# Block transposes on VectorE and moves by DMA in place of TensorE transposes, in the second layer of an attention and two-layer expert kernel

## The chip, the cores and the metric

The kernel runs on one core of a Trainium2 chip. Its time is the device time of one execution in microseconds; the median of three runs is the number that is compared. The engines of the core are called TensorE (PE in the profile; PEld is its loading of stationary operands), VectorE (DVE), ScalarE (ACT), GpSimd (POOL) and SyncE (SP, which here only issues DMAs).

## The reference

A chunked attention (4608 tokens, 8 heads of 64) gives x of 4608 x 512. A first layer with a cosine gate follows, and then the second layer, the one that is changed. All values are float32.

```python
def _moe_ref(x, w_in, w_out):            # 512 -> 2048 -> 512
    h = x @ w_in
    g = h * np.cos(h)
    return (g @ w_out).astype(np.float32)

def _moe2_ref(x, w_in, w_out, g_ln):     # 512 -> 1024 -> 512
    h = x @ w_in
    h_max = np.max(h, axis=-1, keepdims=True)
    e = np.exp(h - h_max)
    sm = e / (np.sum(e, axis=-1, keepdims=True) + 1e-09)
    solu = h * sm
    mu = np.mean(solu, axis=-1, keepdims=True)
    var = np.mean((solu - mu) ** 2, axis=-1, keepdims=True)
    ln = (solu - mu) / np.sqrt(var + 1e-06) * g_ln
    return (ln @ w_out).astype(np.float32)
```

## The kernel before

Products are made of float32 numbers split into a high part `hi` (type float32r) and a low part `lo`; a product is three matmuls, hi by hi, hi by lo, lo by hi. `split` (L115 to L124) makes the high part with a copy on ScalarE and the low part with a subtraction on VectorE.

The attention and the first layer run together in nine blocks of 512 tokens (`NJ` = 9, `T` = 512). The first layer's result y leaves the chip for DRAM (`yd`, L595) and comes back for the second layer (`yr`, L608), with units on partitions and tokens along the row. The second layer's weights are loaded by `load_w2` (L217) and split by `prep_w2` (L228) in the last sixteen steps of the first layer; the gain `gcol`, loaded at L657 among the first loads, is multiplied into the second output weights there (L121, L122).

The second layer goes by tiles of 128 tokens, `NI` = 36 of them, four (`SUB`) to a block. For a tile t:

- `mm_h2(t)` (L812): 24 matmuls make the scores h, 128 tokens on partitions by 1024 units, into one of two two-bank PSUM buffers of `ps_y` (tag y).
- `stats(t)` (L825): on VectorE the maximum `nm` (L829), on ScalarE the exponentials `e` with their sum (L831), on VectorE the units `so` (L836), on ScalarE the sum of squares (L841), on GpSimd the power -1/2 (L846). The last reader of the PSUM buffer is the operation that writes `so`; then `mm_h2(t + 2)` can write it.
- `norm(t)` (L849): one VectorE operation on `so` (L851).
- `mm_t(t)` (L855): eight 128 x 128 transposes of `so` on TensorE into PSUM, `lt` (L861), because the next product needs units on partitions.
- `split_ln(t)` (L864): `lh` and `ll` from `lt`, on ScalarE and VectorE, into tiles of the pool `wp` (32 buffers of 4 KB a partition; the second layer's split weights hold 16 of them).
- `mm_o(t)` (L870): 24 matmuls make 128 tokens by 512 outputs in `ps_h`.
- `store(t)` (L880): a copy on ScalarE, one DMA of 256 KB.

The loop (L887 to L904) writes these in the order `mm_h2(t)`, `norm(t-1)`, `split_ln(t-2)`, `store(t-3)`, `load_y`, `stats(t)`, `mm_o(t-2)`, `mm_t(t-1)`: a tile's output product comes two tiles after its first product. `load_y` (L600) fetches the y of the block after the next one; its destination has two buffers, so it can be split only when the block before the last is through. In this part no order is prescribed for an engine: a planner walks through a simulation of the program and gives each engine the first written operation whose operands and buffers it believes to be ready, and on the chip each engine, SyncE's DMA queue too, keeps the order so found and waits where something is not ready.

Of the kernel before, what the change touches and what calls it, by code (L numbers as in the profile page):

```python
# [11 lines left out]
F32 = mybir.dt.float32  # L12
# [4 lines left out]
AF = mybir.ActivationFunctionType  # L17
# [12 lines left out]
def kernel(  # L30
# [12 lines left out]
    nc = tc.nc  # L43
# [4 lines left out]
    P = 128  # L48
    CH = 64
    T = 512  # L50
    NJ = NT // T
    SUB = T // P
    NI = NT // P
    KD = DM // P
    NF = F1 // P
    NF2 = F2 // P
    NH2 = F2 // 512
# [8 lines left out]
    ps_a = ctx.enter_context(tc.tile_pool(name="ps_a", bufs=1, space=PSUM))  # L66

    ident = const.tile([P, P], F32, name="ident")
    gcol = const.tile([P, NF2], F32, name="gcol")
# [43 lines left out]
    sync = InOrder(nc.sync, in_order_loads)  # L113

    def split(src, hi, lo, mul=None):  # L115

        if mul is None:
            act.activation(out=hi, in_=src, func=AF.Copy)
            dve.tensor_tensor(out=lo, in0=src, in1=hi.bitcast(F32), op=ALU.subtract)
        else:  # L120
            nc.scalar.activation(out=hi, in_=src, func=AF.Copy, scale=mul)  # L121
            nc.vector.scalar_tensor_tensor(  # L122
                out=lo, in0=src, scalar=mul, in1=hi.bitcast(F32), op0=ALU.mult, op1=ALU.subtract
            )  # L124
# [32 lines left out]
    def wtile(dt, name, n=1024):  # L157
        return wp.tile([P, n], dt, tag="w", name=name)
# [13 lines left out]
    def load_one(name, f):  # L172
        t = wtile(U64, "raw", 512)
        load_w(name, f, t)
        raw.setdefault((name, f // 2), []).append(t)

    def load_pair(name, g):
        t = sp_.tile([P, 1024], U64, tag="st", name="st")
        for e in range(2):
            load_w(name, 2 * g + e, t[:, HALVES[e]])  # L180
        raw[name, g] = [t]
# [15 lines left out]
    def prep_split(name, g, e=None):  # L197
        sl = slice(0, 1024) if e is None else HALVES[e]
        if (name, g) not in his:
            his[name, g], los[name, g] = wtile(F32R, "whi"), wtile(F32R, "wlo")  # L200
        split(zs[name, g][:, sl].bitcast(F32), his[name, g][:, sl], los[name, g][:, sl])
        dst = win if name == "in" else wout
        for e in range(2):
            dst[2 * g + e] = tuple(x[name, g][:, HALVES[e]] for x in (his, los))
# [3 lines left out]
    def prep(name, g):  # L208
# [3 lines left out]
        if name == "in" or 2 * g >= N32:  # L212
            prep_split(name, g)

    w2in, w2out = {}, {}

    def load_w2(name, g):  # L217
        t = sp_.tile([P, 1024], U64, tag="st", name="st")
        if name == "in":
            nc.sync.dma_start(out=t, in_=w_in2[g * P:(g + 1) * P, :])  # L220
        else:
            nc.sync.dma_start(
                out=t.rearrange("p (e c) -> p e c", e=2),
                in_=w_out2[2 * g * P:2 * (g + 1) * P, :].rearrange("(e p) c -> p e c", p=P),
            )
        raw[name, g] = t

    def prep_w2(name, g):  # L228
# [371 lines left out]
    def load_y(j, half):  # L600
        if half == 0:
            yh[j] = xp.tile([P, KD, T], F32R, tag="xh", name="yh")
            yl[j] = xp.tile([P, KD, T], F32R, tag="xl", name="yl")
        sl = slice(2 * half, 2 * half + 2)
        ts = []
        for src in y_dram[j]:
            t = sp_.tile([P, 2, T], F32, tag="st", name="yr")
            nc.sync.dma_start(out=t, in_=src[sl].rearrange("m p t -> p m t"))  # L608
            ts.append(t)
        t = ts[0]  # L610
        if len(ts) == 2:
            nc.vector.tensor_tensor(out=t, in0=t, in1=ts[1], op=ALU.add)
        split(t, yh[j][:, sl], yl[j][:, sl])


    def second(r):
        if r < 2:
            load_y(0, r)
        if r == 1:
            load_w2("in", 0)  # L620
        if r < 2 or r % 2:
            return
        g = r // 2 - 1
        order = [("in", x) for x in range(KD)] + [("out", x) for x in range(NF2 // 2)]
        if g < len(order):
            prep_w2(*order[g])
        if g + 1 < len(order):
            load_w2(*order[g + 1])
# [4 lines left out]
    if True:  # L633
# [20 lines left out]
        load_v(SUB)  # L654
        for f in (4, 5):
            load_one("out", f)
        sync.dma_start(out=gcol, in_=g_ln.rearrange("(f p) -> p f", p=P))  # L657
        load_pair("in", 3)

        def tok(i):  # L660
# [98 lines left out]
        for i in range(SUB, NU):  # L759
            j, o = divmod(UNITS[i][0] * CH, T)  # L760
# [48 lines left out]
        sp = ctx.enter_context(tc.tile_pool(name="sp", bufs=2, reuse_waits="tile"))  # L809
        h2ps, solu, nmu, rstd, lnp, lnh, lnl, ops = {}, {}, {}, {}, {}, {}, {}, {}  # L810

        def mm_h2(t):  # L812
            ps = ps_y.tile([P, NH2, 512], F32, tag="y", name="h2")
            j, o = divmod(t, SUB)
            ts = slice(o * P, (o + 1) * P)
            a, b = yh[j][:, :, ts], yl[j][:, :, ts]
            for hh in range(NH2):
                for kk in range(KD):
                    whi, wlo = w2in[kk * NH2 + hh]
                    nc.tensor.matmul(out=ps[:, hh], lhsT=a[:, kk], rhs=whi, start=(kk == 0), stop=False)  # L820
                    nc.tensor.matmul(out=ps[:, hh], lhsT=a[:, kk], rhs=wlo, start=False, stop=False)  # L821
                    nc.tensor.matmul(out=ps[:, hh], lhsT=b[:, kk], rhs=whi, start=False, stop=(kk == KD - 1))  # L822
            h2ps[t] = ps
# [25 lines left out]
        def norm(t):  # L849
            so = solu[t]  # L850
            nc.vector.tensor_scalar(  # L851
                out=so, in0=so, scalar1=nmu.pop(t), scalar2=rstd.pop(t), op0=ALU.add, op1=ALU.mult
            )

        def mm_t(t):  # L855
            so = solu.pop(t).rearrange("p a b -> p (a b)")
            o = ps_a.tile([P, NH2, 4, P], F32, tag="a", name="lt")
            for hh in range(NH2):
                for g in range(4):
                    f = 4 * hh + g  # L860
                    nc.tensor.transpose(out=o[:, hh, g], in_=so[:, f * P:(f + 1) * P], identity=ident)  # L861
            lnp[t] = o

        def split_ln(t):  # L864
            hi, lo = wtile(F32R, "lh"), wtile(F32R, "ll")
            o = lnp.pop(t).rearrange("p a b c -> p (a b c)")
            split(o, hi[:], lo[:])
            lnh[t], lnl[t] = (x.rearrange("p (f c) -> p f c", c=P) for x in (hi, lo))

        def mm_o(t):  # L870
            o = ps_h.tile([P, DM], F32, tag="h", name="o")
            for f in range(NF2):
                a, b = lnh[t][:, f], lnl[t][:, f]
                whi, wlo = w2out[f]
                nc.tensor.matmul(out=o, lhsT=a, rhs=whi, start=(f == 0), stop=False)  # L875
                nc.tensor.matmul(out=o, lhsT=a, rhs=wlo, start=False, stop=False)  # L876
                nc.tensor.matmul(out=o, lhsT=b, rhs=whi, start=False, stop=(f == NF2 - 1))  # L877
            ops[t] = o

        def store(t):  # L880
            s = sp.tile([P, DM], F32, tag="os", name="os")
            nc.scalar.activation(out=s, in_=ops.pop(t), func=AF.Copy)
            nc.sync.dma_start(out=out[t * P:(t + 1) * P, :], in_=s)

        load_y(1, 0)
        load_y(1, 1)
        for t in range(NI + 3):  # L887
            if t < NI:
                mm_h2(t)
            if 0 <= t - 1 < NI:  # L890
                norm(t - 1)
            if 0 <= t - 2 < NI:
                split_ln(t - 2)
            if 0 <= t - 3 < NI:
                store(t - 3)
            if t < NI:
                jn = t // SUB + 2
                if t % SUB >= 2 and jn < NJ:
                    load_y(jn, t % SUB - 2)
                stats(t)  # L900
            if 0 <= t - 2 < NI:
                mm_o(t - 2)
            if 0 <= t - 1 < NI:
                mm_t(t - 1)  # L904


_INS = ["q", "k", "v", "moe_w_in", "moe_w_out", "moe2_w_in", "moe2_w_out", "moe2_g_ln"]
# [24 lines left out]
```

## Time and profile before

| | us |
|---|---|
| median of 3 runs | 1363.74 (1361.95 to 1364.02) |
| profiled execution | 1363.55 |
| its span in the trace | 1361.8 |
| TensorE busy in the span | 1318.3 (97%) |
| VectorE busy | 893.3 (66%) |
| ScalarE busy | 722.2 (53%) |

The table is read from the profiled execution except for its first line. Matmuls are pipelined: one of 512 columns is shown as 390 ns, while at full clock they follow each other every 0.23 us. The second layer begins on TensorE at 928 us. In the trace a name after the line number is the tile that is written, and the names behind the arrow are those that are read; some matmuls carry a wrong tile name among their operands (`whi` for a tile of activations), so the line says which it is.

### The profile page before, as it was taken

How to read it: one execution, taken by the hardware profiler on the slowest of the kernel's cores; microseconds unless marked ns; L12 is line 12 of the kernel's file. 1: busy time of each engine (PE TensorE's matmuls, PEld its weight loads, DVE VectorE, ACT ScalarE, POOL GpSimd, SP SyncE). 2: the span in 40 equal slices, each digit the busy share in tenths (PEclk: the TensorE clock that was granted, in tenths of full speed). 3: DMA queues.
4: the chain of work that ended last, by engine and by line, in shares of the span. 5: the costliest groups of instructions: out<-in, count | busy, mean ns of one | idle time of the engine just before them, and what ended most of it. 6: DMA issues, size and time to landing. Idle time of an engine off the chain costs nothing.

```text
span 1361.8 us, 19898 instructions
## 1 busy us (share of the span) xinstructions
PE 1318.3 (97%) x8048; PEld 1069.0 (78%) x8048; DVE 893.3 (66%) x1326; ACT 722.2 (53%) x1061; POOL 20.5 (2%) x43
## 2 busy tenths in 40 slices
PE   5899999999999999999999999999999999999997
PEld 4566877888888888888888888777888888888886
DVE  4887987666766776677777776997544445444442
ACT  3777886666645554555555455674433344343332
POOL 0000000000000000000000000000000000000000
PEclk9899999999999999999999999999999999999999
DMA  9941343221321221222214003223110111010000
GB/s 239 201 102 62 124 105 66 50 55 22 79 40 23 63 47 31 53 42 46 55 26 105 20 1 115 102 93 124 55 55 24 55 54 55 24 54 18 24 24 31
DMA packets 200172, 87.30 MB, mean 64 GB/s; under 512 B 171408, under 2 KB 179600, under 8 KB 199568
## 3 DMA queue, kind: packets, MB, share of 16 engines
q1 hardware_dynamic: 200080, 86.03, 24.2%
q8 instruction: 63, 1.03, 0.3%
q14 instruction: 29, 0.24, 0.1%
HBM read 65.02 MB, written 20.97 MB: 63 GB/s over the span
## 4 chain that ended last, share of the span: by engine, by line
PE 80%; DVE 9%; ACT 5%; DMA 2%; issue 2%; SPq 1%; POOLq 0%; POOL 0%; ACTq 0%; DVEq 0%
PE h L515 8%; PE y L583 8%; PE y L584 8%; PE h L516 7%; PE y L582 7%; PE h L517 7%; PE o L877 5%; PE o L875 5%; PE o L876 5%; PE h L821 4%; PE h L822 4%; PE h L820 4%; DVE z L105 3%; PE lt L861 2%; PE x L105 2%
## 5 line engine op out<-in xcount | busy, mean ns | idle before, releaser
L515 PE MATMUL h<-xh,whi 128*128 128x512 f32 x576 | 232.6, 404 | 1.0 <-ACT xh L105 1.0
L516 PE MATMUL h<-xl,whi 128*128 128x512 f32 x576 | 226.0, 392 | 1.9 <-DVE xl L105 1.9
L517 PE MATMUL h<-xh,wlo 128*128 128x512 f32 x576 | 226.4, 393 | 0.0
L582 PE MATMUL y<-gh,whi 128*128 128x512 f32 x544 | 211.1, 394 | 10.6 <-ACT gh L105 6.3
L583 PE MATMUL y<-gl,whi 128*128 128x512 f32 x544 | 214.7, 395 | 1.4 <-DVE gl L105 1.3
L584 PE MATMUL y<-gh,wlo 128*128 128x512 f32 x544 | 214.0, 394 | 0.0
L544 ACT ACTIVATE r<-r 128x512 f32<-128x512 f32 x144 | 90.8, 631 | 177.5 <-DVE r L538 177.3
L552 DVE SCALAR_TENSOR_TENSOR hs<-r,hs 128x512 f32<-128x512 f32 x136 | 93.9, 691 | 100.4 <-ACT r L545 100.0
L105 DVE TENSOR_TENSOR gl<-hs,gh 128x512 fp32r<-128x512 f32 x136 | 93.7, 689 | 61.0 <-ACT gh L105 60.7
L582 PEld LDWEIGHTS y<-gh,whi 128*128 128x128 f32 x544 | 102.1, 189 | 35.9 <-ACT gh L105 8.9
L515 PEld LDWEIGHTS h<-xh,whi 128*128 128x128 f32 x576 | 108.9, 189 | 26.2 <-issue 2.2
L516 PEld LDWEIGHTS h<-xl,whi 128*128 128x128 f32 x576 | 108.9, 189 | 25.1 <-DVE xl L105 2.4
L105 ACT ACTIVATE gh<-hs 128x512 fp32r<-128x512 f32 x136 | 85.6, 630 | 80.5 <-DVE hs L552 69.3
L517 PEld LDWEIGHTS h<-xh,wlo 128*128 128x128 f32 x576 | 108.8, 189 | 23.5 <-issue 0.6
L583 PEld LDWEIGHTS y<-gl,whi 128*128 128x128 f32 x544 | 103.1, 189 | 26.1 <-DVE gl L105 4.5
L584 PEld LDWEIGHTS y<-gh,wlo 128*128 128x128 f32 x544 | 103.4, 190 | 21.7 <-DVE wlo L105 0.5
L831 ACT ACTIVATE e<-h,nm 128x1024 f32<-128x1024 f32 x36 | 40.0, 1112 | 144.5 <-DVE nm L829 144.5
L535 DVE SCALAR_TENSOR_TENSOR r<-kt,hs 128x512 f32<-128x512 int32 x144 | 99.4, 690 | 25.2 <-ACT kt L530 21.8
L820 PE MATMUL h<-whi,yh 128*128 128x512 f32 x288 | 114.9, 399 | 0.5 <-DVE so L836 0.5
L875 PE MATMUL o<-whi,lh 128*128 128x512 f32 x288 | 112.3, 390 | 2.2 <-ACT lh L105 2.2
L877 PE MATMUL o<-whi,ll 128*128 128x512 f32 x288 | 112.4, 390 | 1.1 <-DVE ll L105 1.1
L522 ACT ACTIVATE hs<-h 128x512 f32<-128x512 f32 x144 | 85.1, 591 | 53.1 <-PE h L517 44.9
(92 smaller groups left out, 2061.8 us busy)
## 6 DMA issues: line engine op xcount, KB each, us to landing
yd<-ye SPq DMA_DIRECT2D x22, 512.0 KB
yr<-yd SPq DMA_DIRECT2D x22, 512.0 KB
out<-os SPq DMA_DIRECT2D x36, 256.0 KB
vi<-in_v SPq DMA_DIRECT2D x64, 128.0 KB
qi<-in_q SPq DMA_DIRECT2D x224, 32.0 KB
ki<-in_k SPq DMA_DIRECT2D x224, 32.0 KB
st<-in_moe_w_in SPq DMA_DIRECT2D x10, 512.0 KB
st<-in_moe_w_out SPq DMA_DIRECT2D x10, 512.0 KB
```

Of the source, the lines that this page charges most:

```text
L105: ins = getattr(self.engine, name)(*args, **kwargs)
L515: nc.tensor.matmul(out=t, lhsT=wa, rhs=xh[j][:, kk, :], start=(kk == 0), stop=False)
L516: nc.tensor.matmul(out=t, lhsT=wa, rhs=xl[j][:, kk, :], start=False, stop=False)
L517: nc.tensor.matmul(out=t, lhsT=wb, rhs=xh[j][:, kk, :], start=False, stop=(kk == KD - 1))
L535: nc.vector.scalar_tensor_tensor(out=r, in0=kt, scalar=-TWO_PI_HI, in1=h, op0=ALU.mult, op1=ALU.add)
L552: nc.vector.scalar_tensor_tensor(out=gf.get(n, h), in0=rr.pop(n), scalar=-0.5, in1=h, op0=ALU.add, op1=ALU.mult)
L582: nc.tensor.matmul(out=o, lhsT=wa, rhs=a, start=head, stop=False)
L583: nc.tensor.matmul(out=o, lhsT=wa, rhs=b, start=False, stop=False)
L584: nc.tensor.matmul(out=o, lhsT=wb, rhs=a, start=False, stop=last)
L820: nc.tensor.matmul(out=ps[:, hh], lhsT=a[:, kk], rhs=whi, start=(kk == 0), stop=False)
L875: nc.tensor.matmul(out=o, lhsT=a, rhs=whi, start=(f == 0), stop=False)
L877: nc.tensor.matmul(out=o, lhsT=b, rhs=whi, start=False, stop=(f == NF2 - 1))
```

## The change

The eight TensorE transposes of a tile are gone. After `norm(t)`, `blocks32(t)` transposes `so` on VectorE in blocks of 32 x 32: partition 32a + f of the result holds unit f of each of the 32 unit blocks for the 32 tokens of token block a. Four tiles are collected in one tile `bt` (16 KB a partition, one buffer). When the four are complete, `shuffle(j)` moves them with 16 DMAs from SyncE, each from 32 partitions to 32 partitions, 4 KB a row and 128 KB in all: four tiles `lt` arise, each with units on 128 partitions and 128 tokens along the row, taken 32 from each of the four token tiles. `split_ln`, `mm_o` and `store` then work on such a mixed tile (j, a); the split reads SBUF, the output leaves in four DMAs of 32 rows. The units come to lie in another order on the partitions, so the second output weights and the gain are loaded in that order, by four DMAs each in place of one. The output product of a tile comes six tiles after the first product (`LAG2` = 6).

```diff
@@ load_w2 @@
-            nc.sync.dma_start(
-                out=t.rearrange("p (e c) -> p e c", e=2),
-                in_=w_out2[2 * g * P:2 * (g + 1) * P, :].rearrange("(e p) c -> p e c", p=P),
-            )
+            for c in range(4):
+                nc.sync.dma_start(
+                    out=t[32 * c:32 * (c + 1)].rearrange("p (e m) -> p e m", e=2),
+                    in_=w_out2.rearrange("(c q p) m -> c p q m", c=4, p=32)[c, :, 2 * g:2 * g + 2],
+                )
@@ first loads @@
-        sync.dma_start(out=gcol, in_=g_ln.rearrange("(f p) -> p f", p=P))
+        for c in range(4):
+            sync.dma_start(
+                out=gcol[32 * c:32 * (c + 1)],
+                in_=g_ln.rearrange("(c q p) -> c p q", c=4, p=32)[c],
+            )
@@ second layer @@
-        def mm_t(t):
-            so = solu.pop(t).rearrange("p a b -> p (a b)")
-            o = ps_a.tile([P, NH2, 4, P], F32, tag="a", name="lt")
-            for hh in range(NH2):
-                for g in range(4):
-                    f = 4 * hh + g
-                    nc.tensor.transpose(out=o[:, hh, g], in_=so[:, f * P:(f + 1) * P], identity=ident)
-            lnp[t] = o
+        def blocks32(t):
+            j, n = divmod(t, SUB)
+            if n == 0:
+                blks[j] = sp.tile([P, 32, SUB, 32], F32, tag="bt", name="bt", bufs=1)
+            nc.vector.transpose(
+                out=blks[j][:, :, n], in_=solu.pop(t).rearrange("p a (b f) -> p (a b) f", f=32)
+            )
+
+        def shuffle(j):
+            b = blks.pop(j)
+            for a in range(4):
+                l = wtile(F32, "lt")
+                for c in range(4):
+                    nc.sync.dma_start(
+                        out=l[32 * c:32 * (c + 1)],
+                        in_=b[32 * a:32 * (a + 1), 8 * c:8 * (c + 1)].rearrange("p q n t -> p (q n t)"),
+                    )
+                lnp[j, a] = l
...
+        def split_ln(j, a):
             hi, lo = wtile(F32R, "lh"), wtile(F32R, "ll")
+            split(lnp.pop((j, a)), hi[:], lo[:])
...
-        def store(t):
+        def store(j, a):
             s = sp.tile([P, DM], F32, tag="os", name="os")
+            nc.scalar.activation(out=s, in_=ops.pop((j, a)), func=AF.Copy)
+            for n in range(SUB):
+                t0 = j * T + n * P + 32 * a
+                nc.sync.dma_start(out=out[t0:t0 + 32, :], in_=s[32 * n:32 * (n + 1)])
...
-        for t in range(NI + 3):
+        LAG2 = 6
+        for t in range(NI + LAG2 + 1):
             if t < NI:
                 mm_h2(t)
             if 0 <= t - 1 < NI:
                 norm(t - 1)
-            if 0 <= t - 2 < NI:
-                split_ln(t - 2)
-            if 0 <= t - 3 < NI:
-                store(t - 3)
+                blocks32(t - 1)
+                if t % SUB == 0:
+                    shuffle(t // SUB - 1)
+            if 0 <= t - LAG2 + 1 < NI:
+                split_ln(*divmod(t - LAG2 + 1, SUB))
+            if 0 <= t - LAG2 - 1 < NI:
+                store(*divmod(t - LAG2 - 1, SUB))
             if t < NI:
                 jn = t // SUB + 2
                 if t % SUB >= 2 and jn < NJ:
                     load_y(jn, t % SUB - 2)
                 stats(t)
-            if 0 <= t - 2 < NI:
-                mm_o(t - 2)
-            if 0 <= t - 1 < NI:
-                mm_t(t - 1)
+            if 0 <= t - LAG2 < NI:
+                mm_o(*divmod(t - LAG2, SUB))
```

## Rows read from the trace of the kernel before

**Rows 1.** The page's first part: busy time of each engine, share, instructions.
```profile
PE 1318.3 (97%) x8048; PEld 1069.0 (78%) x8048; DVE 893.3 (66%) x1326; ACT 722.2 (53%) x1061; POOL 20.5 (2%) x43
```

**Rows 2.** Stages: length, busy time per engine, granted clock, DMA share, GB/s.
```profile
core 0: us, PE busy (x) PEld busy (x) DVE busy (x) ACT busy (x) POOL busy (x), PEclk, DMA share, GB/s
928.00:1330.00 402.00, 401.18 (x1908) 334.68 (x1907) 197.21 (x333) 152.24 (x226) 18.71 (x35) 1.00 0.13 48
```

**Rows 3.** Chain of waits in the second layer: start, length, what.
```profile
1011.40 0.88 PE lt L861 x8
...
1329.28 0.87 PE lt L861 x8
```

**Rows 4.** Groups by line, 1060 to 1340: busy us, mean ns | idle before.
```profile
L861 PE MATMUL lt<-ident,so 128*128 128x128 f32 x184 | 23.8, 273 | 0.0
```

**Rows 5.** Timeline of VectorE, one tile: start, length, operation, [idle before, releaser].
```profile
1029.54 1.23 DVE L829 TENSOR_REDUCE nm<-h 128x1 f32<-128x1024 f32 x1 [3.17 <-PE h L822]
...
1033.63 0.08 DVE L836 DVE_READ_ACCUMULATOR so<-h,ss,e 128x1 f32 x1
...
1036.17 0.81 DVE L851 TENSOR_SCALAR so<-so,mu,rs 128x1024 f32<-128x1024 f32 x1 [0.73 <-POOL rs L846]
```

**Rows 6.** Line 372, attention: count, shortest/median/longest ns, first and last start.
```profile
L372 DVE STREAM_TRANSPOSE qt<-qi x14: 1235/1236/1240, 162.6 to 769.8; 128x1024 f32<-128x1024 f32 x14
```

**Rows 7.** Groups on VectorE, 1060 to 1340.
```profile
L105 DVE TENSOR_TENSOR ll<-lt,lh 128x1024 fp32r<-128x1024 f32 x24 | 29.3, 1223 | 0.0
L851 DVE TENSOR_SCALAR so<-so,mu,rs 128x1024 f32<-128x1024 f32 x24 | 19.5, 814 | 17.8 <-POOL rs L846 17.8
L105 DVE TENSOR_TENSOR yl<-yr,yh 128x1024 fp32r<-128x1024 f32 x8 | 9.4, 1217 | 0.0
```

**Rows 8.** Timeline of VectorE, a tile in which new activations are split.
```profile
958.90 1.23 DVE L829 TENSOR_REDUCE nm<-h 128x1 f32<-128x1024 f32 x1 [0.84 <-PE h L822]
960.04 2.35 DVE L105 TENSOR_TENSOR yl<-yr,yh 128x1024 fp32r<-128x1024 f32 x2
...
966.44 0.81 DVE L851 TENSOR_SCALAR so<-so,mu,rs 128x1024 f32<-128x1024 f32 x1 [0.73 <-POOL rs L846]
```

**Rows 9.** SyncE's queue: DMA issues by tile (ns), and the second output weights.
```profile
L883 SPq DMA_DIRECT2D out<-os x36: 332/333/351, 954.1 to 1358.8; - x36
L105 SPq DMA_DIRECT2D qi<-in_q x232: 311/449/4488, 23.5 to 731.3; - x116
875.80 30.70 SPq L222 DMA_DIRECT2D st<-in_moe_w_out  x4
```

**Rows 10.** Waits of SyncE's queue: us in total, times, longest.
```profile
SPq L928 <- DMA out<-os: 1.5, 1, 1.5
```

**Rows 11.** Stages with busy DMA engines (columns as in rows 2).
```profile
0.00:10.00 10.00, 3.98 (x44) 3.08 (x44) 1.14 (x2) 3.69 (x5) 0.74 (x7) 1.00 0.81 179
20.00:30.00 10.00, 5.24 (x103) 4.09 (x105) 4.59 (x9) 4.77 (x9) 0.00 (x0) 1.00 1.04 338
40.00:60.00 20.00, 18.10 (x167) 13.73 (x167) 14.22 (x21) 13.84 (x22) 0.00 (x0) 0.82 0.94 232
930.00:936.00 6.00, 6.00 (x28) 4.99 (x27) 2.32 (x3) 0.68 (x1) 0.00 (x0) 1.00 0.77 278
```

**Rows 12.** Timeline of the second layer's begin, TensorE and VectorE.
```profile
928.35 0.39 PE L820 MATMUL h<-whi,yh 128*128 128x512 f32 x1
939.92 0.47 PE L820 MATMUL h<-whi,yh 128*128 128x512 f32 x1 [0.50 <-DVE so L836]
944.37 1.28 DVE L836 SCALAR_TENSOR_TENSOR so<-h,ss,e 128x1024 f32<-128x1024 f32 x1
```

**Rows 13.** Stages at the end of the first layer (columns as in rows 2).
```profile
920.00:925.00 5.00, 2.48 (x9) 1.47 (x8) 3.87 (x6) 2.92 (x4) 0.00 (x0) 0.93 0.00 0
925.00:930.00 5.00, 5.00 (x18) 3.93 (x17) 2.42 (x3) 2.25 (x3) 0.00 (x0) 0.73 0.21 81
```

**Rows 14.** Chain of waits at the end: start, length, what.
```profile
1335.64 1.23 DVE nm L829
...
1357.88 0.24 PE o L877
...
1358.20 0.60 ACT os L882
```

More of the change, by code (lines that the diff above doesn't have):

```diff
@@ L853, in norm @@
             )
-        def mm_t(t):
-            so = solu.pop(t).rearrange("p a b -> p (a b)")
-            o = ps_a.tile([P, NH2, 4, P], F32, tag="a", name="lt")
-            for hh in range(NH2):
-                for g in range(4):
-                    f = 4 * hh + g
-                    nc.tensor.transpose(out=o[:, hh, g], in_=so[:, f * P:(f + 1) * P], identity=ident)
-            lnp[t] = o
-        def split_ln(t):
+        blks = {}
+        def blocks32(t):
[5 more added lines that the diff above has]
+            )
@@ L865, in split_ln @@
+        def shuffle(j):
[9 more added lines that the diff above has]
+        def split_ln(j, a):
             hi, lo = wtile(F32R, "lh"), wtile(F32R, "ll")
-            o = lnp.pop(t).rearrange("p a b c -> p (a b c)")
@@ L867, in split_ln, with mm_o @@
-            split(o, hi[:], lo[:])
-            lnh[t], lnl[t] = (x.rearrange("p (f c) -> p f c", c=P) for x in (hi, lo))
-        def mm_o(t):
+            split(lnp.pop((j, a)), hi[:], lo[:])
+            lnh[j, a], lnl[j, a] = (x.rearrange("p (f c) -> p f c", c=P) for x in (hi, lo))
+        def mm_o(j, a):
             o = ps_h.tile([P, DM], F32, tag="h", name="o")
             for f in range(NF2):
-                a, b = lnh[t][:, f], lnl[t][:, f]
+                hi, lo = lnh[j, a][:, f], lnl[j, a][:, f]
@@ L874, in mm_o @@
                 whi, wlo = w2out[f]
[L875 to L878, printed above, removed]
-        def store(t):
+                nc.tensor.matmul(out=o, lhsT=hi, rhs=whi, start=(f == 0), stop=False)
+                nc.tensor.matmul(out=o, lhsT=hi, rhs=wlo, start=False, stop=False)
@@ L881, in store @@
+                nc.tensor.matmul(out=o, lhsT=lo, rhs=whi, start=False, stop=(f == NF2 - 1))
+            ops[j, a] = o
+        def store(j, a):
             s = sp.tile([P, DM], F32, tag="os", name="os")
-            nc.scalar.activation(out=s, in_=ops.pop(t), func=AF.Copy)
-            nc.sync.dma_start(out=out[t * P:(t + 1) * P, :], in_=s)
+            nc.scalar.activation(out=s, in_=ops.pop((j, a)), func=AF.Copy)
+            for n in range(SUB):
+                t0 = j * T + n * P + 32 * a
+                nc.sync.dma_start(out=out[t0:t0 + 32, :], in_=s[32 * n:32 * (n + 1)])
```

## The prediction

> **What bounds the kernel now.** I read the page's busy shares first, then the stages, then the chain of waits inside the last stage, because the change touches nothing but the second layer and a few early loads. TensorE is busy 97% of the span [rows 1]. From 928 to 1330 us, which is nearly all of the second layer, it is busy 401.2 of 402 us at full clock, while VectorE has work for half of that and the DMA engines for 13% [rows 2]. So here a token tile costs what TensorE needs for it. The chain of waits gives that cost: the eight transposes of a tile start at 1011.40 and, 27 tiles later, at 1329.28 [rows 3], so a tile takes (1329.28 - 1011.40) / 27 = 11.774 us, and of this the transposes hold 0.873 us of the chain. (By the groups a transpose lasts 273 ns [rows 4]; eight of these are 2.2 us, but they overlap, so the chain's figure is the one to use.) Without transposes a tile is 10.90 us.
>
> The other figure to read is the slack around it. The statistics of a tile run from the maximum on VectorE at 1029.54 to the normalisation at 1036.17 [rows 5], 6.63 us over VectorE, ScalarE and GpSimd, one after the other. Here this fits easily into 11.77 us.
>
> **The change part by part.**
>
> *Transposes off TensorE.* 36 tiles x 0.873 us = 31.4 us less on the engine that sets the time. This is the whole gain; the remaining parts say how much of it is given back.
>
> *Transpose on VectorE.* The trace has this very operation elsewhere, 128x1024 float32 in 1.24 us [rows 6]. VectorE's work for a tile becomes about 5.3 + 1.2 = 6.5 us, plus 0.6 for its share of the loaded activations, of 10.90: by busy time alone no bound. By order it is closer. The program writes normalisation, block transpose, low part of the split and then the next maximum, in that order, so the loop from one maximum to the next is 6.63 + 0.81 + 1.24 + 1.22 = 9.9 us [rows 5 to 7]. Once in four tiles the new activations are split in between and the same stretch takes 7.54 instead of 6.63 us (958.90 to 966.44) [rows 8]. Four tiles need 4 x 9.9 + 0.9 = 40.5 us of this loop against 4 x 10.90 = 43.6 us of TensorE: 3.1 us to spare, if nothing else waits. That the split now reads SBUF instead of PSUM I cost at nothing: the split of the activations, which reads SBUF, takes 1.217 us against 1.223 [rows 7].
>
> *The wait for the block tile.* This is the costly new part. There is one such tile, 16 KB a partition. The first transpose of the next four tiles cannot write it until all 16 transfers of the group have read it: 16 x 128 KB = 2.10 MB. What is queued behind that waiting instruction on VectorE is the low part of the split and the whole statistics of the running tile, and behind those TensorE, which may not overwrite a score tile (two buffers) before VectorE has used it. From the end of one group's last transpose to the end of the next one's first, the loop needs S = 0.1 (wake SyncE) + 0.35 (first issue) + 1.5 (landing) + 2.10 MB / rate + 0.2 + 1.24. SyncE needs some 0.33 to 0.45 us for an issue, so 16 issues, 5 to 7 us, are not the limit; the landing figure is the wait for the last output [rows 9, 10]. In place of a 9.9 us loop there stands S, so a group takes S + 30.6 us, and TensorE remains the bound while S is below 13.0.
>
> The rate is not in the trace: nothing there moves SBUF to SBUF on 32 partitions. Bounds are the fastest and the slowest busy stretch, 338 GB/s (20 to 30 us) and 179 GB/s (0 to 10 us); the nearest is 40 to 60 us, where the loads on 64 partitions run with the weights, 232 GB/s at 94% DMA share [rows 11]. At 338 S is 9.6 us, at 232 it is 3.4 + 9.0 = 12.4, at 179 it is 15.1. I take 232: no loss in the steady state. Above 13.0 each us of S costs 7.25 groups x 1 us, and one more in the fill: 179 GB/s would cost 7.25 x 2.1 + 2.7 = 18 us.
>
> The Trainium skill (SBUF — State Buffer, "Door 1: The DMA port swizzle") says that 32 partitions reach half of the memory's ports, measured at 189 GB/s for 1 MiB and 218 at best. By that the transfers would need an estimated 9.6 to 11.1 us and the sum would be 1 to 14 us higher. No run here shows it yet.
>
> *The fill.* The output product now runs six tiles behind the first product instead of two, so at the start TensorE has only 5.45 us of work a tile and follows VectorE. Now it waits 0.5 us there before the third tile [rows 12]. In the new kernel I count 0.5 before the third tile, as before; 1.6 before the fourth (its buffer is free when the second tile's units are done, 945.65 now [rows 12], 1.24 us later with a transpose ahead of it, while TensorE is through at 945.4); 1.8 before the fifth, by the same count; 1.0 each for the next two (6.5 us of VectorE against 5.45). (By this count the units of tile 3 are done at 960.3, those of tile 4 at 966.6.) Then the first transpose of the second group blocks: tile 3 is normalised 2.5 us after its units (1033.7 to 1036.17 [rows 5]) and transposed 0.81 + 1.24 us later, near 964.9, S later is 977.3, the first low part follows at 978.7, and TensorE has been idle since 972.3 (5.45 us after the buffer of tile 4 came free): 6.4 us. Together 12.3 us. An idle stretch of this kind also takes the clock down: after 920 to 925 us, where TensorE was idle for half of the time, the granted clock was 0.73 on average over the next 5 us, so for part of them at the lower of its levels (1.2 and 2.4 GHz): 18 matmuls stand there where 22 fit, 0.9 us [rows 13]. For a longer gap I allow twice that, 1.8 us. Fill: 14.1 us. Bounds: 4 (VectorE's order turns out better) and 20 (S at 179 GB/s and a second fall of the clock).
>
> *The tail.* After the last first product (1335.64) the kernel before still has three output products and two sets of transposes, and then it waits for the splits of the last tiles. The new one has seven output products, 7 x 5.45 us. The last group is needed after three of them, 16.3 us; its path is 6.63 + 0.81 + 1.24, then SyncE and landing 1.95, a quarter of the data 2.3, the high part 1.03 and the low part 1.22, with small gaps some 15.5 to 16.5 us [rows 5 to 7, 10, 14]. I allow 0.5 us. The last output leaves in four transfers instead of one: three more issues, + 1 us, less 0.3 for the smaller transfer.
>
> *Parts that are hidden.* The gain column by four transfers instead of one puts three issues, 1.2 us, into SyncE's early queue ahead of weights and attention loads; TensorE works on older data there (90% busy from 40 to 60 us [rows 11]): 0, at most 1.3. The four loads of the second output weights become sixteen, each on 32 partitions; by the issue times each is sent about 10 us ahead of its use [rows 9], against 3.4 + 1.05 MB / 232 GB/s = 7.9 us: 0, at most 2 if they are halved in rate. Stores: 16 more issues in four tiles, 5 of 43 us of SyncE.
>
> *Sum.* Second layer on TensorE: begin 928.35 [rows 12], 36 x 10.90 = 392.4, fill 14.1, tail 0.5, end 1335.4. Before: 1358.1, with 423.9 of work and 5.9 idle [rows 14]. After TensorE's end 3.7 us now, 4.4 then: span 1339.8 against 1361.8, that is - 31.4 + 8.7 + 0.7. The profiled execution took 1363.55 us, 1.75 over its span and 0.2 below the median of 1363.74. 1339.8 + 1.75 = 1341.5 us.
>
> **Rivals.**
> *No wait at all.* The program's planner orders each engine by when it believes operands to be ready. If it believes the transfers to be as slow as they are, it puts the blocked transpose behind the next maximum and nothing stalls. Then the 6.4 and 1.8 us go, and up to 4 of the rest: 1329 to 1333 us. For it: in the trace yl is placed behind the maximum although it is written ahead [rows 8]. Against it: yl waits for TensorE there, and I see no row in which the planner foresaw a transfer.
> *Narrow transfers at half rate: slower.* If a transfer that reads 32 partitions and writes 32 gets half of what one on 128 gets, the rate is 169 to 139 GB/s (half of 338 and of 278 [rows 11]) and S 15.8 to 18.5. The loop over VectorE with its wait becomes the bound: 7.25 x (2.8 to 5.5) + 3.4 to 6.1 = 24 to 46 us back, 1365 to 1387 us. It decides from 172 GB/s downwards (S 15.6). For it: all four transfers of a quarter read the same 32 partitions, and outputs in 32-partition pieces join the same queue. Against it: stretches with 64-partition loads reach 232 GB/s.
> *Just even.* A rate a little above that, or smaller losses in each group (clock falls, semaphore waits ahead of the transposes), about 20 us in all: 1358 to 1365 us.
>
> **How the numbers follow.** Forecast 0.54, with its own range 1333 to 1357; no wait 0.15; half rate 0.22; even 0.09. The predicted time is the forecast's. Range 1329 to 1365: it takes in the forecast's bounds, the first rival and the even case, and leaves out the half-rate case. About 0.2% is what a measurement of this kernel can tell from no change: faster by more 0.73, within 0.05, slower 0.22.
>
> **What would show it.** Right: transposes gone from TensorE, a tile period of 10.9 us in the steady state, block transposes of 1.24 us on VectorE, idle time ahead of every fourth one of 2 to 3 us put down to the DMAs, one TensorE gap of 5 to 7 us near 972 us. Half rate: a group of four tiles takes over 46 us and TensorE waits for the units (so) in every group. No wait: no idle time ahead of the transposes. The forecast is wrong if the four-tile period is not 43.6 us, whatever the total.

## The result and the profile after

| | before | after |
|---|---|---|
| median of 4 runs, us | 1362.85 (1359.93 to 1364.02) | 1349.55 (1347.75 to 1351.49) |
| ratio, 95% interval | | 0.9906 [0.9889, 0.9923] |
| profiled execution, its span | 1363.55, 1361.8 | 1349.91, 1348.1 |
| TensorE busy in the span | 1318.3 | 1292.5 |
| second layer on TensorE, begin to end | 928.35 to 1358.1 | 928.96 to 1343.3 |
| the same, length | 429.8 | 414.4 |

The kernel became 13 us faster, and 21 to 22 had been forecast. The second layer holds the difference: 15.4 us shorter on TensorE, where 22.7 had been forecast (429.8 to 407.0). In the changed kernel the first product is L826 to L828, the output product L895 to L897, the block transpose L870, the moves L879, the stores L905.

First the page's busy times (against [rows 1]) and the rows of the two new operations: count, shortest, median and longest time in ns, first and last start.

```profile
PE 1292.5 (96%) x7760; PEld 1041.8 (77%) x7760; DVE 933.0 (69%) x1362; ACT 723.7 (54%) x1061; POOL 20.5 (2%) x43
L870 DVE STREAM_TRANSPOSE bt<-so x36: 1201/1240/1248, 949.2 to 1308.7; 128x1024 f32<-128x1024 f32 x36
L879 SPq DMA_DIRECT2D lt<-bt x144: 513/589/2089, 970.8 to 1319.4; - x144
```

288 matmuls are gone (8048 to 7760), and the block transpose takes 1.24 us, as in the attention [rows 6]. An issue of a move takes 0.59 us where 0.33 to 0.45 was put.

Next the steady state by windows (columns as in [rows 2]) and the last windows, where the clock was low.

```profile
1043.00:1086.00 43.00, 43.00 (x190) 35.39 (x190) 26.29 (x43) 17.76 (x26) 2.19 (x4) 1.00 0.37 96
1086.00:1129.00 43.00, 43.00 (x191) 35.37 (x190) 26.66 (x42) 16.66 (x24) 2.19 (x4) 1.00 0.37 96
945.00:949.00 4.00, 4.00 (x10) 3.13 (x11) 3.28 (x9) 2.50 (x5) 0.56 (x1) 0.50 0.49 177
1315.00:1318.00 3.00, 3.00 (x9) 2.32 (x8) 1.22 (x1) 1.36 (x2) 0.00 (x0) 0.52 0.93 216
```

In the middle TensorE is busy all of the time at full clock, with twice the DMA traffic of before (96 against 48 GB/s). At 945 us and 1315 us it runs at the lower of its two levels (1.2 GHz): ten matmuls in 4 us. Those places lie behind waits. These are TensorE's waits in the second layer, from its timeline (start, length, operation, [idle before, releaser]); the only one left out is 0.43 us at 1287.88.

```profile
944.88 0.77 PE L826 MATMUL h<-whi,yh 128*128 128x512 f32 x1 [4.77 <-DVE so L842]
959.79 0.47 PE L826 MATMUL h<-whi,yh 128*128 128x512 f32 x1 [1.38 <-DVE so L842]
972.10 0.47 PE L826 MATMUL h<-whi,yh 128*128 128x512 f32 x1 [1.16 <-DVE so L842]
987.16 0.56 PE L895 MATMUL o<-whi,lh 128*128 128x512 f32 x1 [3.90 <-ACT lh L105]
988.42 0.79 PE L897 MATMUL o<-whi,ll 128*128 128x512 f32 x1 [0.27 <-DVE ll L105]
1313.39 0.50 PE L895 MATMUL o<-whi,lh 128*128 128x512 f32 x1 [1.63 <-ACT lh L105]
1314.65 0.50 PE L897 MATMUL o<-whi,ll 128*128 128x512 f32 x1 [0.53 <-DVE ll L105]
```

A measure that takes in waits and low clock alike makes all kernels of this study comparable. At full clock successive matmuls start 0.227 us apart; what lies above that, summed over the second layer, is its loss. Counted so from each timeline, in four places: ahead of the first output product, at it (the wait before it and the 6 us from its start), the middle, and the tail from 1295 us on.

| kernel | length | ahead | first output | middle | tail | loss |
|---|---|---|---|---|---|---|
| forecast | 407.0 | 5.9 | 8.2 | 0 | 0.5 | 14.6 |
| after | 414.4 | 10.5 | 6.1 | 1.0 | 4.3 | 21.9 |
| natural | 413.0 | 8.7 | 6.5 | 1.0 | 4.3 | 20.5 |
| split_earlier | 408.0 | 8.6 | 6.4 | 0 | 0.9 | 15.9 |
| first_split_pinned | 401.6 | 8.6 | 0 | 0 | 1.0 | 9.6 |
| wide_moves | 403.2 | 8.6 | 0 | 0 | 2.5 | 11.1 |
| interleaved | 412.3 | 8.6 | 6.4 | 0 | 5.2 | 20.2 |
| sum_on_gpsimd | 400.8 | 7.8 | 0 | 0 | 0.9 | 8.7 |
| two_queues | 437.2 | 8.4 | 6.5 | 20.5 | 9.4 | 44.8 |
| transposed_twice | 434.3 | 10.7 | 6.8 | 20.5 | 3.9 | 42.0 |

The length less the loss is 392.0 to 392.5 us in every row: the 36 tiles of two products. So the work is what was forecast, and nearly the whole error sits in the losses. Lengths are the better measure here, because the begin of the second layer shifts as well: 928.96 us in after, 924.95 in natural, 930.34 in sum_on_gpsimd, 926.60 to 927.57 in the other six; a difference of two medians holds such a shift too. The rest of this text asks what makes each.

### The profile page after: what moved, and what is told of

It reads as the page before. It is cut to its first block, busy times and chain, and to the rows that moved or that the text cites. A ratio compares the mean times of both kernels' runs of the same rounds, so it can differ in the third digit from the quotient of the medians.

```text
span 1348.1 us, 19875 instructions
## 1 busy us (share of the span) xinstructions
PE 1292.5 (96%) x7760; PEld 1041.8 (77%) x7760; DVE 933.0 (69%) x1362; ACT 723.7 (54%) x1061; POOL 20.5 (2%) x43
## 4 chain that ended last, share of the span: by engine, by line
PE 77%; DVE 12%; ACT 6%; issue 2%; SPq 2%; DMA 2%; POOL 0%; ACTq 0%; DVEq 0%; POOLq 0%
PE h L517 8%; PE y L585 7%; PE y L584 7%; PE y L586 7%; PE h L518 7%; PE h L519 7%; PE o L897 5%; PE o L895 5%; PE o L896 5%; PE h L826 4%; PE h L827 4%; PE h L828 4%; DVE z L105 4%; SPq L105 2%; PE x L105 1%
## 5 line engine op out<-in xcount | busy, mean ns | idle before, releaser
L826 PE MATMUL h<-whi,yh 128*128 128x512 f32 x288 | 113.4, 394 | 7.3 <-DVE so L842 7.3
L895 PE MATMUL o<-whi,lh 128*128 128x512 f32 x288 | 113.7, 395 | 5.5 <-ACT lh L105 5.5
L897 PE MATMUL o<-whi,ll 128*128 128x512 f32 x288 | 113.6, 395 | 1.2 <-DVE ll L105 0.8
L896 PE MATMUL o<-wlo,lh 128*128 128x512 f32 x288 | 113.4, 394 | 0.0
```

The costliest lines, as they stand in the source:

```text
L895: nc.tensor.matmul(out=o, lhsT=hi, rhs=whi, start=(f == 0), stop=False)
L896: nc.tensor.matmul(out=o, lhsT=hi, rhs=wlo, start=False, stop=False)
L897: nc.tensor.matmul(out=o, lhsT=lo, rhs=whi, start=False, stop=(f == NF2 - 1))
```

## The experiments

Three theories for the 7 us that are missing. *Order*: operations that TensorE needs stand on VectorE or ScalarE behind work for other tiles, or behind an operation that itself waits for TensorE; then an edit of the order alone brings the time back. *Transfers*: the narrow moves are late; then faster moves bring it back, and an edit of the order doesn't. *VectorE full*: then less work there helps and more of it hurts at once. Each kernel below is an edit of natural, the first one, or of a successor of it.

### The weights in their old order (natural)

In the trace of after the third tile waits 4.77 us (944.88 above). The chain of waits leads from there back through the operations on `z` and `wlo`, the last preparation of the second layer's output weights, on VectorE:

```profile
931.83 1.23 DVE L596 TENSOR_SCALAR ye<-y 128x1024 f32<-128x1024 f32 x1 [4.09 <-DMA yd<-ye]
932.98 1.41 DVE L105 TENSOR_SCALAR z<-z 128x1024 f32<-128x1024 f32 x2
...
937.70 1.42 DVE L122 SCALAR_TENSOR_TENSOR wlo<-z,gcol,whi 128x512 fp32r<-128x512 f32 x2 [0.79 <-ACT whi L121]
939.23 2.36 DVE L835 TENSOR_REDUCE nm<-h 128x1 f32<-128x1024 f32 x2
```

The first tile's maximum comes at 939.23; in the kernel before it came at 934.02:

```profile
934.02 1.23 DVE L829 TENSOR_REDUCE nm<-h 128x1 f32<-128x1024 f32 x1 [2.92 <-PE h L822]
```

Two things make it late. The preparation (932.98 to 939.1) stands ahead of it, and VectorE had stood still for 4.09 us before that, at `ye`, the second half of the last y, until the first half was stored in DRAM. The loaded weights, `ye` and `yr` share the two buffers of one pool (`st`); the last weights, not yet prepared, held one of them.

This kernel writes the 32 x 32 blocks in another order, so that the moves leave the units in their natural order and the weights and the gain column are loaded as before.

```diff
-                out=blks[j][:, :, n], in_=solu.pop(t).rearrange("p a (b f) -> p (a b) f", f=32)
+                out=blks[j].rearrange("p (c q) n t -> p q c n t", c=4)[:, :, :, n],
+                in_=solu.pop(t).rearrange("p a (b c f) -> p (a b) c f", c=4, f=32),
```

> The block transposes write the 32 unit blocks in another order, so that the second output weights and the gain are loaded as in the kernel before (one DMA each on 128 partitions); all else as in the changed kernel. Theory A (the narrow weight loads make the planner push the last weights' preparation behind the first layer's end, which keeps the buffers of y and makes the third tile wait 4.8 us and the clock fall): the wait before the third tile is under 2 us, no clock fall there, 1342 to 1345 us. Rival B (the third tile waits because VectorE has the block transposes and the six-tile lag to serve): the wait of 4.8 us stays, 1348 to 1350 us.

Measured: 1345.27 us (1341.74 to 1346.81) beside 1363.51 of the kernel before, ratio 0.9866 [0.9839, 0.9893], just above the 1342 to 1345 of theory A. TensorE's timeline at the same place:

```profile
936.39 0.47 PE L821 MATMUL h<-whi,yh 128*128 128x512 f32 x1 [0.26 <-DVE so L837]
946.96 0.77 PE L821 MATMUL h<-whi,yh 128*128 128x512 f32 x1 [4.89 <-DVE ss L834]
```

The wait of the third tile is gone (0.26 us), so the split loads had caused it, by what they do to the order on VectorE and to the buffers of `st`. But a wait of the same size stands one tile later, ahead of the fourth; the loss ahead of the first output product falls only from 10.5 to 8.7. Of the 5.4 us by which the span is shorter than that of after (1342.7 and 1348.1) the second layer's length gives only 1.4; the other 4.0 are its earlier begin, of which the six successors of natural with a begin near 927 show only 1.4 to 2.4. Ahead of the fourth tile VectorE has work almost without a pause:

```profile
937.36 1.22 DVE L830 TENSOR_REDUCE nm<-h 128x1 f32<-128x1024 f32 x1
...
940.58 1.25 DVE L865 STREAM_TRANSPOSE bt<-so 128x1024 f32<-128x1024 f32 x1
941.75 1.18 DVE L613 TENSOR_TENSOR yr<-yr 128x1024 f32<-128x1024 f32 x1
...
942.92 1.21 DVE L830 TENSOR_REDUCE nm<-h 128x1 f32<-128x1024 f32 x1
944.06 1.23 DVE L105 TENSOR_TENSOR yl<-yr,yh 128x1024 fp32r<-128x1024 f32 x1
...
945.53 1.27 DVE L837 SCALAR_TENSOR_TENSOR so<-h,ss,e 128x1024 f32<-128x1024 f32 x1
```

Between the second tile's maximum (937.36) and its units (945.53), on which TensorE waits, stand a block transpose, the sum of a loaded y, the next maximum and a split: 5 us of work for other tiles. So this wait fits both *VectorE full* and *order*: whether the units placed ahead of that work would have ended it was not tried. In the kernel before TensorE had output products and transposes to do in this stretch.

### The moves: rate or issue (wide_moves, interleaved, two_queues)

Three kernels, each one edit of natural, ask what the 16 moves of a group cost. The first moves each quarter with one DMA over 128 partitions, with the same bytes; the exchange across partitions is left out.

```diff
-                for c in range(4):
-                    nc.sync.dma_start(
-                        out=l[32 * c:32 * (c + 1)],
-                        in_=b[32 * a:32 * (a + 1), 8 * c:8 * (c + 1)].rearrange("p q n t -> p (q n t)"),
-                    )
+                nc.sync.dma_start(
+                    out=l, in_=b[:, 8 * a:8 * (a + 1)].rearrange("p q n t -> p (q n t)")
+                )
```

> As natural, but each quarter is moved by one DMA from 128 partitions to 128 partitions, the same bytes without the shift across partitions (so the units come to the wrong partitions: the move across partitions is left out). Theory A (port width: a transfer on 32 partitions goes at some 200 GB/s): in the tail the quarters land about 1.5 us apart instead of 2.5, the wait for the first low part in the fill shrinks from 4.2 us to under 2, and the total falls 3 to 6 us below natural. Rival B (the waits in fill and tail come from the order the planner gave ScalarE, not from the transfers' speed): quarters land sooner, but the fill wait changes only if the order does; total within 2 us of natural.

The second issues the moves of the four partition quarters in turn (`for r`, then `a in (0, 2, 1, 3)` with `c = (r + a) % 4`), so that neighbours in the queue read and write different partitions.

> As natural, but the 16 narrow transfers are issued so that neighbours read from and write to different partition quarters (read quarters 0, 2, 1, 3 in turn). Theory A (each narrow transfer is held by the ports of its own 32 partitions): all 16 land in 7 to 9 us after the first issue instead of 12. Rival B (SyncE's 0.55 to 0.65 us an issue sets the pace, or the DMA engines do): still 11 to 12 us. In both cases the first quarter lands late, since all four complete together; total 0 to 4 us above natural.

The third issues every other move from ScalarE.

```diff
-                    nc.sync.dma_start(
+                    (nc.scalar if c % 2 else nc.sync).dma_start(
```

> As natural, but every second of the 16 narrow transfers is issued from ScalarE's queue instead of SyncE's. Theory A (the pace of issue, 0.63 us for each transfer of 32 rows, sets the 12 us of a group): issuing takes some 5 us and the last quarter lands 7 to 9 us after the first issue. Rival B (the transfer itself goes at some 200 GB/s whoever issues it): the last quarter still lands 11 to 12 us after the first issue. The total may fall by 0 to 4 us, or rise, since ScalarE's own work waits behind its issues.

Measured: wide_moves 1336.88 us (1333.89 to 1337.97), ratio 0.9804 [0.9784, 0.9825]; interleaved 1345.71 (1343.26 to 1348.00), 0.9872 [0.9851, 0.9893]; two_queues 1370.98 (1369.19 to 1373.42), 1.0060 [1.0039, 1.0081]. The last group of each is the cleanest place to look, because nothing else moves then but outputs: windows of after, wide_moves, interleaved and two_queues, in this order.

```profile
1312.00:1320.00 8.00, 6.08 (x18) 4.54 (x19) 3.67 (x3) 4.06 (x5) 0.00 (x0) 0.79 0.89 205
1300.00:1305.00 5.00, 3.15 (x13) 1.92 (x12) 2.33 (x3) 3.86 (x5) 0.00 (x0) 1.00 0.98 396
1307.00:1314.00 7.00, 5.36 (x22) 4.13 (x23) 1.23 (x1) 1.06 (x2) 0.00 (x0) 1.00 0.91 207
1327.00:1333.00 6.00, 0.47 (x3) 0.04 (x1) 0.00 (x0) 0.00 (x0) 0.00 (x0) 0.91 0.96 216
```

The DMA engines are busy for 89 to 98% in all four. With 32 partitions they move 205 to 216 GB/s, whatever the order and the number of issuing queues; with 128 partitions the same bytes move at 396. The number of issues isn't the limit: from two queues 16 issues take 8.7 us, from one 10.05, and the rate stays. So the long issues of after wait for the transfers. One rival is left: wide_moves has not only wider moves but also four of 512 KB in place of sixteen of 128 KB, and no run changes the size alone. Pauses between transfers can't be the difference, as the engines are busy for 89 to 96% with the narrow moves.

That the width of a move sets the rate is what the Trainium skill (SBUF — State Buffer, "Door 1: The DMA port swizzle") states, with 189 GB/s for 32 partitions at 1 MiB and 218 at best; 205 to 216 GB/s here agree. It also says ("Can I just issue two DMAs to hit both halves?") that two transfers on different halves serialize; 207 GB/s of interleaved agrees.

Yet the 8.4 us by which wide_moves beats natural aren't the rate's alone, and they are more than was expected. Of the lost time 6.5 us lay at the first output product and are gone, and there no transfer had been waited for (next experiment). In wide_moves ScalarE splits the moved units first and the new activations `yh` later; with fewer moves the planner chose another order:

```profile
971.30 2.95 ACT L105 ACTIVATE lh<-lt 128x1024 fp32r<-128x1024 f32 x3
985.35 2.01 ACT L105 ACTIVATE yh<-yr 128x1024 fp32r<-128x1024 f32 x2 [0.95 <-PE h L822]
1302.69 0.50 PE L889 MATMUL o<-whi,lh 128*128 128x512 f32 x1 [1.63 <-ACT lh L105]
```

Only the tail, 4.3 to 2.5 us, can be the rate's directly, and even there the wait of 1.63 us that after has is still found (last row).

two_queues shows the price of the wrong queue. ScalarE stands at its issues (five of the eight of a group in these 6.89 us), and TensorE behind it, in the middle too (20.5 us):

```profile
1003.25 6.89 ACTq L875 DMA_DIRECT2D lt<-bt  x5
1010.24 1.06 ACT L105 ACTIVATE lh<-lt 128x1024 fp32r<-128x1024 f32 x1 [11.42 <-DMA lt<-bt]
```

### The tail and the first output product (split_earlier, first_split_pinned)

In the tail of after the wait before L895 ends with `lh`, and `lh` doesn't wait for data. ScalarE's timeline:

```profile
1311.80 0.60 ACT L902 ACTIVATE os<-o 128x512 f32<-128x512 f32 x1 [4.39 <-PE o L897]
1312.29 1.05 ACT L105 ACTIVATE lh<-lt 128x1024 fp32r<-128x1024 f32 x1
1314.32 1.06 ACT L105 ACTIVATE lh<-lt 128x1024 fp32r<-128x1024 f32 x1 [0.98 <-DMA lt<-bt]
```

The copy `os` waits 4.39 us for TensorE to finish a product, and the split that TensorE needs next is queued behind it. The first edit writes the split one tile earlier (on natural):

```diff
-            if 0 <= t - LAG2 + 1 < NI:
-                split_ln(*divmod(t - LAG2 + 1, SUB))
+            if 0 <= t - LAG2 + 2 < NI:
+                split_ln(*divmod(t - LAG2 + 2, SUB))
```

> As natural, but the split of a mixed tile is written two tiles ahead of its output product instead of one. Theory A (in the tail ScalarE has the high part of the last tile of the last group but one queued behind a copy of outputs that waits for TensorE, which costs 2.2 us and a clock fall of 1.8 us): the wait at that place is gone and the total is 3 to 4 us below natural, 1338 to 1341 us. Rival B (the tail waits for the transfers): unchanged within 1 us.

Measured: 1342.13 us (1341.87 to 1345.32), ratio 0.9851 [0.9831, 0.9871]; the tail's loss is 0.9 us after 4.3. The median is 3.1 us below natural, as theory A expected, though not within its 1338 to 1341. TensorE's one wait in the tail, and a window of the last group's moves (columns as in [rows 2]):

```profile
1318.65 0.50 PE L891 MATMUL o<-whi,lh 128*128 128x512 f32 x1 [0.66 <-ACT os L898]
1308.00:1316.00 8.00, 8.00 (x37) 6.62 (x36) 2.92 (x3) 3.18 (x3) 0.00 (x0) 1.00 0.90 206
```

So it was the order, not the transfers: they run as slowly as before (206 GB/s) and ScalarE's splits still wait 1.4 to 1.6 us each for them, but TensorE has products to do meanwhile and stands for 0.66 us only.

The wait at the first output product stays (6.4). Its row in after, on ScalarE:

```profile
983.07 2.00 ACT L105 ACTIVATE yh<-yr 128x1024 fp32r<-128x1024 f32 x2 [2.69 <-PE h L827]
984.98 1.10 ACT L837 ACTIVATE e<-h,nm 128x1024 f32<-128x1024 f32 x1
...
986.07 2.94 ACT L105 ACTIVATE lh<-lt 128x1024 fp32r<-128x1024 f32 x3
```

Three `lh` run one after the other without waiting for data: their moves had landed. ScalarE stood at `yh`, whose buffer TensorE was still reading (2.69 us), and then TensorE stood for `lh`, queued behind `yh` and `e`. The second edit, on split_earlier, holds the two loads of y that are written at the seventh and eighth tiles, with their splits, and the statistics of the eighth tile behind the first split, in the order handed to the planner (`behind` holds what stands inside it behind the two operations of that split):

```diff
+                with ExitStack() as first_out:
+                    if t in (LAG2, LAG2 + 1):
+                        behind(first_out, (0, 0))
                     if t % SUB >= 2 and jn < NJ:
                         load_y(jn, t % SUB - 2)
+                    if t == LAG2 + 1:
+                        stats(t)
+                if t != LAG2 + 1:
                     stats(t)
```

> As split_earlier, but in the fill the next block's activations and the statistics of the eighth tile are held, in the order of issue, behind the first mixed tile's split, on ScalarE and VectorE. Theory A (the first quarter has landed by then, and TensorE's wait of 3.9 + 0.5 us before the first output product comes from the order in which ScalarE had its work): that wait falls below 1 us with its clock fall, total 3 to 6 us below split_earlier, 1336 to 1339 us. Rival B (the quarter lands late): the wait stays and the total is the same or higher.

Measured: 1335.70 us (1332.10 to 1335.81), ratio 0.9793 [0.9775, 0.9810], some 14 us faster than after. It has the lowest median here, though wide_moves and sum_on_gpsimd can't be told from it. `lh` now comes before `yh`, and the loss at the first output product is zero. ScalarE's rows there, and then all that TensorE still waits for in the second layer:

```profile
976.66 1.05 ACT L105 ACTIVATE lh<-lt 128x1024 fp32r<-128x1024 f32 x1
979.51 1.06 ACT L105 ACTIVATE yh<-yr 128x1024 fp32r<-128x1024 f32 x1 [1.80 <-PE h L823]
```

```profile
938.97 0.47 PE L822 MATMUL h<-whi,yh 128*128 128x512 f32 x1 [0.53 <-DVE so L838]
949.54 0.77 PE L822 MATMUL h<-whi,yh 128*128 128x512 f32 x1 [4.89 <-DVE ss L835]
968.56 0.47 PE L822 MATMUL h<-whi,yh 128*128 128x512 f32 x1 [0.37 <-DVE so L838]
1312.27 0.50 PE L896 MATMUL o<-whi,lh 128*128 128x512 f32 x1 [0.73 <-ACT os L903]
```

### What is left at the begin (sum_on_gpsimd)

The fourth tile's wait is in every version so far with the weights in natural order, at 4.85 to 4.89 us. To take work off VectorE there, the sum of the two loaded halves of y goes to GpSimd:

```diff
-            nc.vector.tensor_tensor(out=t, in0=t, in1=ts[1], op=ALU.add)
+            nc.gpsimd.tensor_tensor(out=t, in0=t, in1=ts[1], op=ALU.add)
```

> As first_split_pinned, but the sum of the two halves of y of the first two blocks (1.22 us each, four of them, two in the second layer's first tiles) is made on GpSimd. Theory A (in the fill VectorE's own work, which now has the block transposes, makes the fourth tile wait 4.9 us): that wait falls by 1 to 3 us and the total by 1 to 5 us. Rival B (the wait before the fourth tile comes from transfers or ScalarE): no change or up to 3 us more, because GpSimd takes longer for a sum.

Measured: 1337.56 us (1333.36 to 1339.12), ratio 0.9808 [0.9787, 0.9829], no different from 1335.70. The fourth tile's wait fell by 2.6 us, as theory A expected, but the total didn't: now the sixth tile waits 2.81 us for the fourth tile's statistics (the row is in the last section), and the loss ahead of the first output product only goes from 8.6 to 7.8.

```profile
949.85 0.66 PE L822 MATMUL h<-whi,yh 128*128 128x512 f32 x1 [2.31 <-DVE so L838]
```

The second layer began at 930.3 where it had begun at 927.3; whether the edit caused that, one profile can't tell. Inconclusive: 7.8 us or more ahead of the first output product stay in every changed kernel, and what would bring them back is open.

### VectorE's margin (transposed_twice)

VectorE is busy for 61% of the steady state, and there the block transpose costs nothing. Is that a wide margin? On natural, each block transpose is made twice.

> As natural, but each block transpose is made twice into the same place: 1.24 us more for VectorE in each tile. Theory A (the prediction's loop: one maximum after the next in a fixed order, 9.9 us, would become 11.1 us against 10.9): the steady state loses some 0.2 us a tile, with the fill 9 to 14 us above natural. Rival B (the planner interleaves, so only busy time counts, 7.7 of 10.9 us): the steady state stays at 10.9 us a tile and only the fill grows, 1 to 6 us above natural.

Measured: 1368.36 us (1365.67 to 1370.41), ratio 1.0038 [1.0027, 1.0049]: 23 us more than natural, against the 9 to 14 and 1 to 6 that the two theories expected; both missed. Of the loss, 20.5 us are in the middle. One of its places, on ScalarE and TensorE:

```profile
1026.77 2.00 ACT L105 ACTIVATE yh<-yr 128x1024 fp32r<-128x1024 f32 x2 [2.75 <-PE h L822]
1028.67 1.10 ACT L832 ACTIVATE e<-h,nm 128x1024 f32<-128x1024 f32 x1
...
1029.76 3.89 ACT L105 ACTIVATE lh<-lt 128x1024 fp32r<-128x1024 f32 x4
1030.86 0.50 PE L893 MATMUL o<-whi,lh 128*128 128x512 f32 x1 [3.90 <-ACT lh L105]
```

This is the pattern of the first output product, now at the change of a group: `yh` waits for TensorE, `lh` stands behind it, TensorE waits for `lh`. It recurs near 1123 and 1218 us, every second group. So 1.24 us more a tile isn't paid as VectorE's busy time (28.3 of 43 us, the mean of six stretches) but through an order in which two engines wait for each other. Why the planner orders it so, and whether the time comes back when that order is pinned, was not tried.

## Why the prediction was right and where it wasn't

*The gain, right.* 31.4 us off TensorE and 10.90 us a tile were the forecast. First products that lie one group of four tiles apart start at 1087.44, 1131.15 and 1174.67 in after: 43.7 and 43.5 us, against 43.6. In first_split_pinned, where nothing disturbs the middle, 27 tiles take (1284.18 - 990.42) = 293.76 us, 10.88 each. The block transpose is 1.24 us and hidden.

*The wait for the block tile, wrong.* The step assumed that VectorE keeps the written order and stands at every fourth transpose for 2 to 3 us. No row of after has such a wait. VectorE's and SyncE's timelines around one group show why:

```profile
1049.33 10.05 SPq L879 DMA_DIRECT2D lt<-bt  x16
1069.15 4.63 DVE L105 TENSOR_TENSOR ll<-lt,lh 128x1024 fp32r<-128x1024 f32 x4 [0.36 <-ACT lh L105]
1073.70 2.36 DVE L870 STREAM_TRANSPOSE bt<-so 128x1024 f32<-128x1024 f32 x2
```

The moves are issued from 1049.33 to 1059.4. The next group's first transpose comes only at 1073.70, behind the four low parts, with the second one right behind it. The planner put it there, though the first of the two tiles had been normalised at 1056.03. This is the first rival's mechanism ("No wait at all", 0.15), and the argument against it, that no row showed the planner foreseeing a transfer, was too weak a reason to leave it at that. The rate was over-estimated as well: 205 GB/s instead of 232, which by the forecast's own formula gives S = 3.4 + 10.2 = 13.6 us, above the threshold of 13.0. In the written order each group would have lost 0.6 us; so "no loss in the steady state" came out right by luck, not by its reason. The half-rate rival (139 to 169 GB/s) is excluded by the windows.

*The fill, near in size and wrong in place.* 14.1 us were forecast and 10.5 + 6.1 measured; that the sums lie so close is luck, since the two large losses have other causes than those that were put. Ahead of the first output product the terms were 0.5, 1.6, 1.8, 1.0 and 1.0, together 5.9, and no clock in them; measured were 7.3 at the third tile (a gap of 4.9 and 2.3 of low clock behind it), 1.5 and 1.3 later, and small ones. The term that failed is the one for the output weights' loads, "0, at most 2". It asked whether the data come in time. They do; but with sixteen loads the planner moved the preparation of the last weights behind the end of the first layer on VectorE, 932.98 to 939.1, where TensorE was waiting for statistics, and VectorE lost 4.09 us more at `ye` for want of a buffer. Undone in natural, the third tile's wait vanishes; 1.8 us of loss come back, the rest moves to the fourth tile. There the term was mis-sized: 1.6 us allowed for one block transpose ahead of the second tile's units, and 4.89 measured, because the next maximum, a sum and a split stand ahead of them too. The 6.4 + 1.8 us near 972 were put down to a transpose that waits for moves; the gap came at 987 with 3.90 + 0.27 us and low clock, and first_split_pinned shows that ScalarE's order made it.

*The tail, mis-sized.* 0.5 us were allowed, 4.3 lost. The path of the last group was counted as a chain of durations, and nothing in it was queued behind another tile's work. The trace has 1.63 + 0.53 us behind `os`, and some 2 us of low clock after them; split_earlier gives 3.4 of it back.

*The sum.* The second layer began 0.6 us later than put, lost 21.9 instead of 14.6, and had 4.8 us after TensorE's end instead of 4.4: 8.3 us over the predicted span of 1339.8, which is the measured 1348.1. With the order mended, first_split_pinned comes 5.8 us below the forecast.

## What to carry to other kernels

Taking work off the engine that sets the time gave what the chain of waits said, to 0.03 us a tile. What is given back lies at the places where the pipeline fills, changes groups and drains, and there it was mostly the order in the queues that decided: ask of each operation that the bound engine needs what stands ahead of it on its own engine, and whether that waits for the bound engine. A new operation that fits by busy time, or more and smaller loads that arrive in time, can still change the order that a planner makes, so its place should be read from the trace, and pinned if it is wrong.

## What the runs showed of the hardware

Moves inside SBUF between 32 partitions and 32 others run at 205 to 216 GB/s with all DMA engines busy, those between 128 and 128, in transfers four times as large, at 396 GB/s. An issue from SyncE took 0.59 us while the moves were in the way, against 0.33 for an output of before [rows 9].

A block transpose writes its 32 x 32 blocks in another order at no cost: natural's and after's both take 1.24 us.

The clock's fall isn't set by the length of a wait alone. After 4.77 us (945 us, after) the granted clock was 0.50 for 4 us, and after 1.63 + 0.53 (1315 us) 0.52 for 3; but in sum_on_gpsimd, where it was 0.58 from 950 to 954 us behind the wait of 2.31 us, a wait of 2.81 us at 965.41 left it at full level:

```profile
965.41 0.47 PE L822 MATMUL h<-whi,yh 128*128 128x512 f32 x1 [2.81 <-DVE ss L834]
965.00:970.00 5.00, 4.59 (x20) 3.86 (x21) 4.13 (x12) 2.66 (x6) 0.55 (x1) 1.00 0.01 3
```

Here the second row's clock column is 1.00. What makes the difference stays open.
